# Moving the loads, casts and scores of an attention tail within a one-core kernel

## The chip, the core and the metric

The kernel runs on one core of a Trainium2 chip. The metric is device time in microseconds, the median of several runs. The core has five engines with a queue of their own each: TensorE (PE, with its weight loads as PEld), VectorE (DVE), ScalarE (ACT), GpSimd (POOL) and SyncE (SP). SyncE computes nothing here: it issues nearly all the DMAs, one after the other. Engines meet only by semaphores, so an instruction that waits holds up everything behind it on its engine.

## The reference

For 8 batches of 576 positions with 8 heads of 64 columns, the kernel computes sliding window attention and then a two-layer network with a residual:

```python
rel = pos[:, None] - pos[None, :]
mask = (rel >= 0) & (rel < 64)
scores = np.where(mask, q @ k.T / 8, -1e9)          # per batch and head
x = softmax(scores) @ v                              # (8, 576, 512) over all heads
xn = (x - mean(x)) / sqrt(var(x) + 1e-6) * g_ln
out = x + relu(xn @ w_ch1) @ w_ch2                   # 512 -> 2048 -> 512
```

## The kernel before

**Groups.** Rows go through the network in nine groups of 512. Groups 0 to 7 are the first 512 positions of batches 0 to 7. Group 8 (`NGRP - 1`) holds what is left, the last 64 positions of each batch. These are handled in four *tails* of two batches each; tail i belongs to batches 2i and 2i+1 and gives block i of group 8.

**A period.** The loop over `g` emits the network of group g (`mlp_units`) and, between its units, the attention of group g+1 and the loads and casts of group g+2. A unit is a piece of TensorE work: for g = 2 to 6 units 0 to 15 are layer 1 (one 128-row slice of the hidden layer each, `l1`, L498 and L502), units 16 to 29 are layer 2 as seven products of a Strassen scheme in two halves each (`stage`, in the order 4, 1, 2, 6, 5, 7, 3; L572). `at(i, f, ...)` puts a call behind unit i; calls behind the same unit run in the order in which `at` was called, and `at(40, ...)` means behind the last unit. So the order on every engine's queue is the order of these calls, written out by hand. No scheduler changes it.

**Attention of a block.** `load_qk` loads, `cast_qk` casts to 16 bits on GpSimd (or `cast_act` on ScalarE), `t_main` transposes (q of later batches by a DMA transpose from SyncE, L275, k on TensorE, L286), `s_pe` computes scores (L345), `s_exp` exponentiates (L355), `s_mask` multiplies by the mask on VectorE (L365), `b_pe` multiplies with v (L392), `b_rows` divides, writes the rows `xn` (L412, L416) and takes their statistics (L422, L425), `z_step` normalizes on GpSimd (L444 to L450), and `zt_step` transposes z into zT by a DMA transpose from SyncE (L470). `after_mask` (L358) is a one-element copy on GpSimd that reads a masked tile, so that GpSimd's later work waits for that mask product.

**A tail.** `load_tail` loads q (L107), k and v (L110); `cast_tail` casts q and k (L117, L118), `cast_tail_v` v (L124); `t_tail` transposes both by DMA (L302, L303). Scores and values run through the same `s_pe`, `s_exp`, `s_mask`, `b_pe` with group number 8.

**Around layer 2.** `s_sums` (L546) makes the Strassen sums sS of hidden rows on VectorE, in pieces of chunks. `post` (L585) and `post_both` (L581) add a product's bank into `xn`. Product 6 continues in the bank of product 1, so it waits for `post("A", 0, 0)`. `store` (L533) writes two blocks of `xn` behind product 7 and two behind product 3, the last two units. `xn` has four buffers of two blocks, so the first rows of group g+1 go where group g-1 was, and wait for its stores.

**Where the change lies.** In periods g = 3 to 6. In the kernel before, tail g-2 is loaded in period g (q and k behind unit 17, v at the end), q and k are cast behind unit 24, transposed by DMA at the end, and scored in period g+1 behind unit 13 (in g = 6 behind unit 9).

Of the kernel before, what the change touches and what calls it, by code (L numbers as in the profile page):

```python
# [18 lines left out]
def kernel(  # L19
# [15 lines left out]
    NGRP = B + 1  # L35
# [927 lines left out]
    for g in range(NGRP):  # L963
# [4 lines left out]
        units, s_sums = begun.get(g) or mlp_units(g, (8, 16, 16)[g] if g < 3 else 0, g == 0, g > 0)  # L968
        slots = [[] for _ in range(len(units) + 1)]

        def at(i, f, *a):
            slots[min(i, len(slots) - 1)].append((f, a))

        def first_scores(b, i):
            at(i, s_pe, b, 0)
            at(i, s_pe, b, 1, False, "xps")
            at(i, s_exp, b, 0, 0, 1)
            at(i + 1, s_exp, b, 1, 0, 1)
            at(i + 1, s_mask, b, 0)
            at(i + 2, s_mask, b, 1)  # L980
# [50 lines left out]
        if g == 1:  # L1031
# [38 lines left out]
            for j in range(4):  # L1070
                i = (13, 16, 22, 22)[j]
# [5 lines left out]
                i = (13, 17, 25, 27)[j]  # L1077
# [26 lines left out]
        if g == 2:  # L1104
            at(0, load_qk, 4, 1)
            at(0, s_exp, 3, 1, 1)
            at(1, z_act, 2, 3)
            at(1, s_mask, 3, 1)
            at(2, b_pe, 3, 0)
            at(2, s_pe, 3, 2)  # L1110
            at(2, s_pe, 3, 3, False, "t")
            at(5, zt_step, 2, 3, "act")
            for i, x in zip((2, 3, 4, 6), ((3, 0), (3, 1), (2, 0), (2, 1))):
                at(i, s_exp, 3, *x)
            at(3, load_v, 4, 0, 4)
            at(4, s_mask, 3, 3)
            at(4, b_rows, 3, 0)
            at(4, z_step, 3, 0)
            at(7, s_mask, 3, 2)
            at(7, alloc_qkT, 4)  # L1120
            at(7, after_mask, 3, 2)
            at(7, cast_qk, 4, 0)
            at(7, cast_qk, 4, 1)
            for j in range(1, 4):
                at(9, b_pe, 3, j, ("xps", "t", "sc")[j - 1])
                at((9, 10, 11)[j - 1], b_rows, 3, j)
                at((9, 10, 11)[j - 1], z_step, 3, j)
            for j, i in enumerate((8, 14, 24, 25)):
                at(i, zt_step, 3, j)
        elif g > 1 and b < B:  # L1130
            r, i = NGRP - 1, g - 3
            x, y = (b, 3), (r, i)
            at(2, b_pe, b, 0)
            at(2, b_rows, b, 0)
            at(2, z_step, b, 0)
            at(2, s_pe, b, 2)
            at(2, s_exp, b, 2, 0, 1)
            at(3, s_mask, b, 2)
            at(2, s_pe, *x, False, "t")
            at(4, s_exp, *x, 0)  # L1140
            at(5, s_exp, *x, 1)
            at(5, s_mask, *x)
            at(7, b_pe, b, 1)
            at(7, b_pe, *x, "t")
            if g == 6:
                at(9, s_mm, *y)
            at(7, b_rows, b, 1)
            at(7, z_step, b, 1)
            if g == 6:
                at(10, s_mask, *y)  # L1150
            at(8, b_rows, *x)
            at(9, z_step, *x)
            at(13, b_pe, b, 2)
            if g == 6:
                at(13, b_pe, *y, "sc")
            else:
                at(13, s_pe, *y)
                at(15, s_exp, *y, 0, 1)
                at(20, s_mask, *y)
            if g + 2 < B:  # L1160
                at(5, alloc_qkT, g + 2)
                at(5, after_mask, *x)
                at(5, cast_qk, g + 2, 0)
                at(5, cast_qk, g + 2, 1, (0,))
                at(15, cast_act, g + 2, 1, 1)
            for j, w in ((13, (b, 2)), (19, y)) if g == 6 else ((17, (b, 2)),):
                at(j, b_rows, *w)
                at(j, z_step, *w)
            at(2, zt_step, b, 0)
            at(14, zt_step, b, 1)  # L1170
            if g == 6:
                at(25, zt_step, r, i)
            at(16, zt_step, b, 3)
            at(18 if g == 6 else 17, zt_step, b, 2)
        n = g + 2
        if g > 1 and n < B:
            if g > 2:
                at(3, load_v, n, 2, 4)
            at(17, alloc_v, n)
            at(17, cast_v, n, 0, 2)  # L1180
            at(17, cast_v, n, 2, 4)
            if g == 2:
                at(26, part_vB, n, 0, 4)
            else:
                at(17, alloc_vB, n)
                for i, f, c in ((18, vB_cur, 0), (18, vB_prev, 0), (19, vB_cur, 1), (19, vB_prev, 1),
                                (24, vB_cur, 2), (24, vB_prev, 2), (24, vB_cur, 3)):
                    at(i, f, n, c, 0)
            for i, (x, half) in zip((13, 18, 13, 22) if g == 2 else (13, 17, 13, 23),
                                    ((0, 0), (1, 0), (0, 1), (1, 1))):  # L1190
                at(i, t_main, n, x, half, 0)
            if g > 2:
                at(23, b_pe, NGRP - 1, g - 3, "sc")
                at(23, b_rows, NGRP - 1, g - 3)
                at(23, z_step, NGRP - 1, g - 3)
            first_scores(n, 27)
            if n + 1 < B:
                for f, a in ((t_tail, (g - 2,)), (load_qk, (n + 1, 0)))[::1 if g == 2 else -1]:
                    at(40, f, *a)
                at(40, load_qk, n + 1, 1)  # L1200
                at(40, load_v, n + 1, 0, 2)
            else:
                at(40, t_tail, g - 2)
            if g > 2:
                at(40, zt_step, NGRP - 1, g - 3)
        if g == 2:
            for c, i in ((0, 13), (4, 16)):
                at(i, s_sums, c, c + 4, 1, 2)
# [1 line left out]
        if 2 < g < NGRP - 2:  # L1210
            for i in range(1, 5):
                at(7 + i, s_sums, 0, 4, i)
                at((13, 13, 18, 19)[i - 1], s_sums, 4, 6, i)
                at((15, 15, 20, 22)[i - 1], s_sums, 6, 8, i)
        if 2 <= g < 6:
            i = g - 2
            for n, part in enumerate("qkv"):
                at(15 if i == 0 else 40 if n == 2 else 17, load_tail, i, part)
            at(24, cast_tail, i)
        if 3 <= g < 7:  # L1220
            at(6 if g == 6 else 16, cast_tail_v, g - 3)
        if g == 5:
# [6 lines left out]
        if g in (6, 7):  # L1229
            i = 25 if g == 6 else 24  # L1230
# [40 lines left out]
```

## Time and profile before

| | us |
|---|---|
| median of three runs | 302.19 |
| the runs | 302.36, 302.19, 300.04 |
| the profiled execution, its own time | 299.51 |
| its span, first to last instruction | 297.8 |
| TensorE busy within the span | 289.3 |
| VectorE busy | 226.7 |
| ScalarE busy | 167.5 |
| GpSimd busy | 166.4 |

The profile is of one execution of the program. "Busy" is the time in which an engine ran at least one instruction, and lines are those of the kernel printed above. `out<-in` names what an instruction writes and reads. In brackets behind a row stand the idle time of the engine just before it and what ended it. For a DMA, the row on SPq is the issue; the landing comes later.

### The profile page before, as it was taken

The numbers are of one execution on the slowest core, as the hardware profiler recorded it, in microseconds if no ns is written. First come the engines' busy times: TensorE is split into PE (matmuls) and PEld (weight loads), VectorE is DVE, ScalarE is ACT, GpSimd is POOL, SyncE is SP. The second block draws the span as 40 slices with busy tenths as digits, with TensorE's granted clock in tenths as the row PEclk, the third lists the DMA queues.
The fourth block names the chain that finished last, engine by engine and source line by source line (L and its number), as shares of the span: only waits on it lengthen the run. The fifth ranks groups of instructions, "written<-read, shape, count | busy, mean of one in ns | idle before, by whom it ended". The sixth has DMA issues, their size and how long they took to land.

```text
span 297.8 us, 7948 instructions
## 1 busy us (share of the span) xinstructions
PE 289.3 (97%) x3207; PEld 210.7 (71%) x3207; DVE 226.7 (76%) x435; ACT 167.5 (56%) x284; POOL 166.4 (56%) x243
## 2 busy tenths in 40 slices
PE   8989999999999999999999999999979999999994
PEld 3558545898888888457854786468634888888883
DVE  2782378799994894498867785779869988988983
ACT  2667667677449625768577757776666117305500
POOL 4688866763850886257746883677456643104300
PEclk9999999999999999999999999999999999999999
DMA  8999999969979999899699999999693222003013
GB/s 189 258 382 341 384 293 285 258 207 299 195 165 274 254 156 216 226 307 170 135 273 272 186 141 279 271 200 189 132 226 69 53 77 84 4 0 144 0 37 106
DMA packets 116519, 57.63 MB, mean 194 GB/s; under 512 B 86273, under 2 KB 107841, under 8 KB 116482
## 3 DMA queue, kind: packets, MB, share of 16 engines
q1 hardware_dynamic: 116112, 56.79, 81.1%
q8 instruction: 25, 0.41, 0.6%
q10 hardware_dynamic: 370, 0.33, 0.3%
q14 instruction: 12, 0.10, 0.1%
HBM read 38.80 MB, written 9.44 MB: 162 GB/s over the span
## 4 chain that ended last, share of the span: by engine, by line
PE 91%; DVE 4%; DMA 1%; ACT 1%; issue 1%; SPq 0%; DVEq 0%
PE hps L498 19%; PE pA L572 14%; PE hph L641 12%; PE pC L572 10%; PE pB L572 9%; PE lA L697 5%; PE xps L392 4%; PE ch L658 4%; PE sc L345 3%; PE tp L286 3%; PE lC L697 2%; PE warm L887 2%; DMA out_dram<-xn 1%; PE ch L510 1%; PE lB L697 1%; PE ztp L474 1%
## 5 line engine op out<-in xcount | busy, mean ns | idle before, releaser
L498 PE MATMUL hps<-zT,w1g 128*128 128x512 f16 x288 | 66.2, 379 | 0.0
L502 ACT ACTIVATE hrT<-hps 128x512 f16<-128x512 f32 x72 | 43.2, 600 | 27.3 <-PE hps L498 22.5
L572 PEld LDWEIGHTS <-sS 128*128 128x128 f16 x512 | 49.1, 98 | 6.5 <-issue 0.5
L498 PEld LDWEIGHTS <-w1g 128*128 128x128 f16 x288 | 27.0, 98 | 30.7 <-issue 1.7
L355 ACT ACTIVATE pt<-sc 128x512 f16<-128x512 f32 x72 | 39.5, 601 | 15.2 <-PE sc L345 14.7
L572 PEld LDWEIGHTS <-hrT 128*128 128x128 f16 x384 | 36.7, 98 | 6.8 <-ACT hrT L502 0.8
L641 PE MATMUL hph<-zT,w1g 128*128 128x256 f16 x320 | 37.9, 273 | 0.0
L161 POOL CAST qk<-qk 128x1024 f16<-128x1024 f32 x26 | 28.0, 1091 | 13.7 <-PE sc L345 5.9
L365 DVE TENSOR_TENSOR pt<-pt,mask 128x1024 f16<-128x1024 f16 x32 | 24.6, 777 | 12.7 <-ACT pt L355 12.7
L641 PEld LDWEIGHTS <-w1g 128*128 128x128 f16 x320 | 30.5, 98 | 4.5 <-ACT w1g L238 0.2
L572 PE MATMUL pC<-w2s,sS 128*128 128x256 f16 x256 | 31.5, 273 | 0.0
L572 PE MATMUL pA<-wT,sS 128*128 128x256 f16 x256 | 30.9, 273 | 0.3 <-DVE xn L585 0.3
L444 POOL TENSOR_SCALAR rsz<-mvg 128x1 f32<-128x1 f32 x32 | 11.0, 342 | 36.1 <-DVE mvg L425 26.3
L646 ACT ACTIVATE hrT<-hph 128x512 f16<-128x512 f32 x40 | 24.1, 606 | 10.9 <-PE hph L641 10.6
L416 DVE TENSOR_TENSOR xn<-xps,rcp 128x256 f32<-128x256 f32 (+1 forms) x50 | 25.7, 538 | 4.7 <-DMA out_dram<-xn 4.1
L714 POOL TENSOR_SCALAR hrT<-hrT 128x512 f16<-128x512 f16 x8 | 12.0, 1503 | 28.5 <-DVE hrT L712 28.5
L546 DVE TENSOR_TENSOR sS<-hrT 128x1024 f16<-128x1024 f16 (+2 forms) x39 | 24.9, 639 | 3.2 <-ACT hrT L502 3.1
L267 ACT COPY qkT<-tp 128x1024 f16<-128x1024 f16 (+1 forms) x18 | 17.4, 965 | 16.0 <-PE tp L286 13.7
L422 DVE BATCH_NORM_STATS2 stats<-xn 128x6 f32<-128x512 f32 x36 | 25.0, 694 | 1.2
L445 POOL TENSOR_TENSOR rsz<-rsz,mhalf 128x1 f32<-128x1 f32 x32 | 21.0, 657 | 2.7
L450 POOL TENSOR_SCALAR z<-xn,rsz 128x512 f16<-128x512 f32 x24 | 20.6, 860 | 2.6 <-DMA zT<-z 0.2
L189 POOL CAST vA<-v 128x1024 f16<-128x1024 f32 (+1 forms) x18 | 17.3, 978 | 5.5 <-DMA v<-in_v_dram 5.4
(115 smaller groups left out, 486.9 us busy)
## 6 DMA issues: line engine op xcount, KB each, us to landing
qk<-in_q_dram SPq DMA_DIRECT2D x16, 512.0 KB, 6.0
qk<-in_k_dram SPq DMA_DIRECT2D x16, 512.0 KB, 6.3
out_dram<-xn SPq DMA_DIRECT2D x32, 256.0 KB, 4.1
v<-in_v_dram SPq DMA_DIRECT2D x28, 256.0 KB, 7.1
w2s<-in_moe_w_ch_dram SPq DMA_DIRECT2D x9, 512.0 KB, 8.4
w1s<-in_moe_w_ch_dram SPq DMA_DIRECT2D x4, 512.0 KB, 7.2
tk<-in_k_dram SPq DMA_DIRECT2D x8, 256.0 KB, 4.3
tv<-in_v_dram SPq DMA_DIRECT2D x8, 256.0 KB, 4.8
```

The costliest lines, as they stand in the source:

```text
L161: nc.gpsimd.tensor_copy(out=dst[:, :].rearrange("p (a j) e d -> p a e j d", j=j), in_=t[:, :].rearrange("p (a e j d) -> p a e j d", e=2, j ...
L355: nc.scalar.activation(out=o, in_=i, func=AF.Exp, bias=0.0, scale=scale)
L365: nc.vector.tensor_tensor(out=ptv, in0=ptv, in1=mb, op=ALU.mult)
L416: nc.vector.tensor_tensor(out=xn[:, n * i:n * i + n], in0=xps[:, :, 0:D], in1=rcp_b, op=ALU.mult)
L422: nc.vector.bn_stats(out=stats, in_=xv)
L498: nc.tensor.matmul(out=hps, lhsT=w1g[:, kc, 128 * hc:128 * (hc + 1)], rhs=zT[g][:, kc, :], start=(kc == 0), stop=(kc == NKC - 1),)
L502: nc.scalar.activation(out=hrT[:, hc, :], in_=hps, func=AF.Relu, bias=0.0, scale=1.0)
L546: nc.vector.tensor_tensor(out=o, in0=x, in1=y, op=op)
L572: nc.tensor.matmul(out=o, lhsT=a[:, c, 128 * p:128 * p + 128], rhs=wv[:, c, :], start=(first and (p == 0 or split_c) and c == 0), stop=(c ...
L641: nc.tensor.matmul(out=hps[:, e], lhsT=w1g[:, kc, 128 * hc:128 * (hc + 1)], rhs=zT[g][:, kc, 256 * half:256 * half + 256], start=(kc == 0) ...
L646: nc.scalar.activation(out=hrT[:, 2 * i:2 * i + 2, 256 * half:256 * half + 256], in_=hps, func=AF.Relu, bias=0.0, scale=1.0)
L697: nc.tensor.matmul(out=o[:, r, :], lhsT=a[:, kc, 2 * d + r, :], rhs=b[:, kc, :], start=(n in (1, 2, 5) and r == 0 and kc == 0), stop=(kc = ...
```

## The change

Tails 1 to 3 (tail 0 stays) are handled one step later. q and k of a tail are loaded behind the stores at the end of a period, ahead of the next q/k loads, and not ahead of the stores; at the end of g = 5 v as well. Their cast and transpose move to the next period behind unit 2, after z of block 0. The zT transpose of the tail block before goes there too. The load of the next v (first half) and of the tail's v move from the end of a period to behind unit 2 of the next. A tail's scores come behind unit 17 in place of 13, ahead of the k transposes (in g = 6 behind 13 in place of 9, with its value product behind 18). A cast of q (second half) on GpSimd goes from unit 5 to 11. One piece of the sum sS number 3 goes from unit 18 to 19, so it stands behind the add of product 1.

```diff
         elif g > 1 and b < B:
             r, i = NGRP - 1, g - 3
             x, y = (b, 3), (r, i)
+            if g > 3:
+                at(2, zt_step, r, i - 1)
             at(2, b_pe, b, 0)
             at(2, b_rows, b, 0)
             at(2, z_step, b, 0)
+            if g > 3:
+                at(2, cast_tail, i)
+                at(2, t_tail, i)
+                if g < 6:
+                    at(2, load_v, g + 2, 0, 2)
+                    at(2, load_tail, i, "v")
...
-            if g == 6:
-                at(9, s_mm, *y)
...
-            if g == 6:
-                at(10, s_mask, *y)
...
+            i_s = 13 if g == 6 else 17
+            at(i_s, s_pe, *y)
+            at(i_s + 2 if g == 6 else i_s, s_exp, *y, 0, 1)
             if g == 6:
-                at(13, b_pe, *y, "sc")
+                at(15, s_mask, *y)
+                at(18, b_pe, *y, "sc")
             else:
-                at(13, s_pe, *y)
-                at(15, s_exp, *y, 0, 1)
                 at(20, s_mask, *y)
...
-                at(5, cast_qk, g + 2, 1, (0,))
+                at(11, cast_qk, g + 2, 1, (0,))
...
             if n + 1 < B:
-                for f, a in ((t_tail, (g - 2,)), (load_qk, (n + 1, 0)))[::1 if g == 2 else -1]:
-                    at(40, f, *a)
+                if g == 2:
+                    at(40, t_tail, 0)
+                else:
+                    at(40, load_tail, g - 2, "q")
+                    at(40, load_tail, g - 2, "k")
+                at(40, load_qk, n + 1, 0)
                 at(40, load_qk, n + 1, 1)
-                at(40, load_v, n + 1, 0, 2)
+                if g == 2:
+                    at(40, load_v, n + 1, 0, 2)
             else:
-                at(40, t_tail, g - 2)
-            if g > 2:
-                at(40, zt_step, NGRP - 1, g - 3)
+                for part in "qkv":
+                    at(40, load_tail, g - 2, part)
...
-                at((13, 13, 18, 19)[i - 1], s_sums, 4, 6, i)
+                at((13, 13, 19, 19)[i - 1], s_sums, 4, 6, i)
...
         if 2 <= g < 6:
             i = g - 2
-            for n, part in enumerate("qkv"):
-                at(15 if i == 0 else 40 if n == 2 else 17, load_tail, i, part)
-            at(24, cast_tail, i)
+            if i == 0:
+                for part in "qkv":
+                    at(15, load_tail, i, part)
+                at(24, cast_tail, i)
```

## The prediction

> **What bounds the kernel now.** I read the page's busy shares first, then busy time by stretches, then TensorE's waits, then the timeline around each wait. A group is a "period" of some 31 us: 16 units of layer 1, then 14 units of layer 2. g=4 runs from 149.8, g=5 from 180.8, g=6 from 212.3.
>
> ```profile
> PE 289.3 (97%) x3207; PEld 210.7 (71%) x3207; DVE 226.7 (76%) x435; ACT 167.5 (56%) x284; POOL 166.4 (56%) x243
> ...
> 149.99:180.96 30.97, 30.97 (x354) 20.59 (x352) 23.12 (x48) 21.73 (x38) 19.79 (x29) 1.00 1.10 215
> 180.96:212.26 31.30, 30.96 (x352) 20.51 (x351) 25.24 (x50) 21.55 (x38) 21.40 (x30) 1.00 1.10 218
> 212.26:243.00 30.74, 28.97 (x301) 18.64 (x299) 25.72 (x53) 12.89 (x24) 16.14 (x24) 1.00 0.52 114
> 243.00:268.00 25.00, 24.96 (x227) 21.85 (x225) 22.06 (x40) 9.24 (x17) 6.05 (x4) 1.00 0.12 43
> ```
>
> ```profile
> PE xps L392 <- DVE pt L365: 1.8, 1, 1.8
> PE pA L572 <- DVE xn L585: 0.3, 1, 0.3
> ```
>
> The columns of the stretches are length, then busy time of PE, PEld, DVE, ACT and POOL, then clock, DMA share and GB/s. TensorE sets the time, at a granted clock of 1.00. Period g=4 has no idle TensorE time at all. Period g=5 is 0.34 us short (31.30 against 30.96 busy), g=6 1.77 us short, and after 243 there is 0.04 us in 25. Matmuls are not removed by this change, so what it can gain in the periods it touches ends at 0.34 + 1.77 = 2.1 us. That is under 1% of the time. About 1% is also what a measurement of this kernel can tell from no change, since the three runs shown lie 2.3 us apart.
>
> **The large wait, 1.77 us in g=6.**
>
> ```profile
> 210.50 1.22 DVE L581 TENSOR_TENSOR xn<-pA,xn 128x1024 f32<-128x1024 f32 x1
> 211.63 1.25 SPq L110 DMA_DIRECT2D tk<-in_k_dram  x2
> 212.98 2.75 SPq L533 DMA_DIRECT2D out_dram<-xn  x4
> 215.47 0.21 DVE L412 RECIPROCAL rcp<-xps 128x8 f32<-128x8 f32 x1 [0.58 <-PE xps L392]
> 218.06 0.69 DVE L416 TENSOR_TENSOR xn<-xps,rcp 128x512 f32<-128x512 f32 x1 [2.39 <-DMA out_dram<-xn]
> 219.31 0.62 ACT L355 ACTIVATE pt<-sc 128x512 f16<-128x512 f32 x1
> 221.93 0.68 DVE L365 TENSOR_TENSOR pt<-pt,mask 128x1024 f16<-128x1024 f16 x1
> 222.67 0.22 PE L392 MATMUL xps<-vB,pt 128*64 128x65 f16 x1 [1.77 <-DVE pt L365]
> ```
>
> Group 5's result is complete at 211.72 (210.50 + 1.22). SyncE is then still issuing tail loads and gives the first store at 212.98. VectorE's multiply for the next group needs the stored buffer, and waits 2.39 us for that landing. Everything behind it on VectorE is late, the last mask product ends at 222.61, and TensorE waits for that one.
>
> After the change the stores come first: 212.98 - 211.72 = 1.26 us earlier. They also no longer queue behind four fresh loads. I take 2.4 us off the multiply (the whole wait; lower bound 1.26). The mask product would then end near 222.61 - 2.4 = 220.2, if its exponent allows. That exponent ends at 219.93 (219.31 + 0.62), so the product ends at 220.6 at the earliest. TensorE wants it at 222.67 - 1.77 = 220.9. So 1.77 us goes with a margin of 0.3 us; at the lower bound 1.26 us goes. Next late would be that exponent.
>
> **The small wait, 0.34 us in g=5.**
>
> ```profile
> 170.91 0.39 DVE L546 TENSOR_TENSOR sS<-hrT 128x512 f16<-128x512 f16 x1
> ...
> 201.69 1.04 POOL L124 CAST vt<-tv 128x1024 f16<-128x1024 f32 x1 [1.41 <-DMA tv<-in_v_dram]
> ...
> 201.88 1.13 DVE L546 TENSOR_TENSOR sS<-hrT 128x512 f16<-128x512 f16 x1
> 202.93 0.68 DVE L585 TENSOR_TENSOR xn<-pA,xn 128x512 f32<-128x512 f32 x1
> ...
> 203.66 1.91 PE L572 MATMUL pA<-wT,sS 128*128 128x256 f16 x16 [0.34 <-DVE xn L585]
> ```
>
> The half sum took 0.39 us in g=4 and 1.13 us in g=5, where GpSimd's cast of the tail's v ran at the same time. The add behind it came late and TensorE waited. With the half sum behind the add, the add starts 1.05 us earlier (202.93 - 201.88). The 0.34 us goes, and nothing waits for that half sum until product 7, four units on. I count -0.34.
>
> **What is moved on TensorE: dearer by 0.1 us a period.** The tail's 16 score matmuls leave a place between layer-1 matmuls and come between layer-2 products and transposes.
>
> ```profile
> 133.37 0.41 PE L345 MATMUL sc<-tqT,tkT 64*128 64x64 f16 x16
> 133.71 1.90 PE L498 MATMUL hps<-zT,w1g 128*128 128x512 f16 x8
> ...
> 143.90 1.92 PE L572 MATMUL pC<-w2s,sS 128*128 128x256 f16 x16
> 145.66 1.91 PE L572 MATMUL pA<-wT,sS 128*128 128x256 f16 x16
> 147.50 0.64 PE L345 MATMUL sc<-qkT,qkT 64*128 64x64 f16 x32
> ```
>
> From start to start the scores cost 0.34 us where they stand (133.71 - 133.37). At the new place the step from 128x256 products into scores is dearer: a product ahead of scores holds 1.84 us (147.50 - 145.66), one ahead of a product 1.76. That is 0.08 a period, in g=3, 4 and 5. In g=6 the tail's 16 value matmuls also lose their neighbours of the same form, of the same order. Sum +0.3; bounds 0 and 0.7 (the scores' 0.34 twice).
>
> **What is moved on GpSimd: the tail casts get between z and the mask product.** Before, the one-element copy that waits for the last mask product stands between z of block 0 and the next casts. Now two tail casts stand ahead of that copy.
>
> ```profile
> 156.64 0.76 POOL L450 TENSOR_SCALAR z<-xn,rsz 128x512 f16<-128x512 f32 x1
> 157.53 0.69 DVE L365 TENSOR_TENSOR pt<-pt,mask 128x1024 f16<-128x1024 f16 x1 [2.04 <-ACT pt L355]
> 158.27 0.20 PE L392 MATMUL xps<-vB,pt 128*64 128x65 f16 x1
> ...
> 148.78 0.61 POOL L117 CAST tq<-tq 128x512 f16<-128x512 f32 x1 [0.85 <-DMA tq<-in_q_dram]
> ...
> 183.75 1.04 POOL L118 CAST tk<-tk 128x1024 f16<-128x1024 f32 x1 [0.99 <-DMA tk<-in_k_dram]
> ```
>
> GpSimd is free at 157.40, the mask product starts at 157.53, ends at 158.22, and TensorE uses its result at 158.27: a margin of 0.05 us. The g=5 half sum showed what a GpSimd cast does to such a VectorE operation: it holds it until the cast is over. If the q cast of 0.61 us gets in first, the product ends about 0.5 us late and TensorE waits as long; if the product gets in first, nothing is lost. The two starts lie 0.1 us apart, so I count half of three periods, 3 x 0.5 / 2 = about +0.7 us; bounds 0 and 3 x (0.61 + 1.04) = 5.0, when both casts get ahead.
>
> [...]
>
> **What is moved on SyncE and the DMA queue: the transposes get tighter.**
>
> ```profile
> 150.00:175.00 25.00, 25.00 (x274) 15.48 (x273) 18.83 (x41) 17.22 (x31) 17.04 (x25) 1.00 1.23 238
> 175.00:180.00 5.00, 5.00 (x73) 4.31 (x72) 3.60 (x8) 3.55 (x7) 2.75 (x6) 1.00 0.48 101
> ...
> 177.18 1.29 SPq L107 DMA_DIRECT2D tq<-in_q_dram  x2
> ...
> tq<-in_q_dram SPq DMA_DIRECT2D x8, 128.0 KB, 3.1
> ...
> L303 SPq DMA_TRANSPOSE tkT<-tk x1: 2713/2713/2713, 154.3 to 154.3; - x1
> DMA to landing us min/median/max: 5.7/5.7/5.7
> ...
> L470 SPq DMA_TRANSPOSE zT<-z x1: 1216/1216/1216, 175.9 to 175.9; - x1
> DMA to landing us min/median/max: 2.3/2.3/2.3
> ...
> 168.25 0.61 PE L286 MATMUL tp<-ident,qk 128*128 128x128 f16 x8
> ```
>
> Before, the four tail loads ran in the quiet end of a period (share 0.48). Now they stand at the head of the busy 25 us (1.23). Issued from 177.18, the last one let GpSimd's cast start at 183.75; taking off the 3.1 us that a single q load takes to land, they hold the queue some 3.5 us. The tail's k transpose landed at 160.0 (154.3 + 5.7). In front of it now come these 3.5 us and two more q/k loads, 1.05 MB at 238 GB/s, 4.4 us at most. It lands at 168 or earlier; TensorE scores the tail at 168.25 - 0.34 = 167.9. So it is close: I take 0 for the likeliest, since the stores ahead land sooner than before; bounds 0 and 1 us in each of g=4 and g=5. Queued behind it on SyncE are the v loads, the group's q transposes and its zT. Before, the last zT of g=4 landed at 178.2 (175.9 + 2.3), 2.6 us ahead of the next period's first product at 180.8; later loads eat into that as well. On ScalarE a cast of k now waits for the same transpose; it stands after layer 1's last evacuation, so only the q/k copies are behind it.
>
> The remaining edits cost nothing that I can find. The second q cast goes from unit 5 to unit 11 of GpSimd's queue, and its transpose is used behind unit 27; the tail's v load moves within the queue; tail 0 is loaded as before.
>
> **Sum** against the profiled execution (299.51 us, span 297.8): -1.77 - 0.34 + 0.3 + 0.7 + 0 = -1.1, so 298.4. The median of the runs shown, 302.19, lies 2.7 above that execution. I carry the same -1.1 to it: 301.1.
>
> **Rivals.**
> - *Nothing collides* (the mask product gets the port first each time): -2.1 + 0.3 = -1.8, 300.4. For it speaks that the cast also needs its q landed and the two starts lie 0.1 us apart; against it the 0.05 us margin.
> - *Both casts ahead of the mask product, the slower side.* Place: around 8 us into g=4, 5 and 6. Price 1.65 us each, 5.0 in all, minus 1.8: +3.2, 305.4. It decides from 0.6 us a period on. For it: GpSimd's second cast follows its first at once if k has landed. Against: a waiting VectorE operation should get its turn between two casts.
> - *The tail transposes come late* (1 us in g=4 and g=5 each): -1.8 + 0.7 + 2 = +0.9, 303.1. Decided by a landing past 167.9.
> - *The change doesn't do what it says:* the store wait goes, but mask or exponent stays as late, so only 0.3 of the 2.1 goes and the 1.0 of costs stays: 302.9.
>
> **Chances.** Forecast (-0.5 to -1.7) 0.45, nothing collides 0.2, late transposes 0.15, both casts ahead 0.1, no gain 0.1. Over 1% faster needs 3 us, more than all idle time there is; only spread of the runs gives it: 0.05. Over 1% slower: the port rival and a part of the late transposes, 0.12. Within 1%: 0.83. The range reaches from the full gain with runs like the lowest (300.04 - 1.8 = 298.2) up to between the late transposes and the port rival, 304.0.
>
> **What would show it.** TensorE's wait for the mask product at the start of g=6 gone or under 0.5 us; no VectorE wait for a store in xn<-xps; the half sum behind the add and no wait of pA. A wait of TensorE for the mask product some 8 us into g=4 and g=5, with a long mask product beside the tq cast, shows the port. A wait at the tail's scores for the transposes, or at a period's first layer-1 matmul for zT, shows the DMA queue. The forecast is wrong if either is over 0.7 us a period.

## The result, and the profile after

In the first comparison the changed kernel took 299.24 us (median of 15 executions, 298.63 to 300.96), the kernel before 301.86 (15 executions, 300.04 to 303.62). The ratio is 0.9923, 95% interval 0.9901 to 0.9945, so it is 0.8% or some 2.3 us faster (2.6 us by the medians). Ratios here leave out executions over 1.5% above the fastest of the same kernel; of the kernel before that takes out 23 of 112 in the groups below, all at a mean granted clock of 0.994 or less. The forecast was 301.1, range 298.2 to 304.0.

The two profiled executions compare the wrong way round: that of the changed kernel was the slowest of its 15 (300.96), that of the kernel before (299.51) was faster than any of its 15. So the profile after shows where time goes, not how much goes in a typical execution. Busy time by periods in the changed kernel, from each period's first layer-1 matmul to the next (columns as in the prediction):

```profile
149.68:183.65 33.97, 31.73 (x355) 20.63 (x353) 24.56 (x50) 22.03 (x38) 19.12 (x30) 1.00 1.09 209
183.65:215.48 31.83, 31.46 (x353) 20.64 (x353) 24.82 (x49) 21.69 (x37) 20.36 (x30) 1.00 1.08 224
215.48:243.35 27.87, 27.75 (x291) 17.64 (x290) 25.64 (x53) 12.54 (x23) 15.53 (x25) 1.00 0.64 128
```

The waits have changed places. Before, g=4 had no idle TensorE time and g=6 had 1.77 us; now g=4 has 2.24 us (33.97 - 31.73), g=5 0.37, g=6 0.12. TensorE's waits say for what:

```profile
PE sc L345 <- DMA qkT<-qk: 1.3, 2, 0.8
...
PE hps L498 <- issue: 0.6, 1, 0.6
...
PE sc L345 <- DMA tkT<-tk: 0.3, 1, 0.3
```

The first and the third are DMA transposes. The second is a period's first layer-1 matmul, which needs zT: the profile names no releaser, but the last zT transpose of g=4 is issued at 181.2 and these take 2.3 to 2.5 us to land, and the matmul starts at 183.65. The waits for the mask product at the start of g=6 and for the add of pA are gone. The timeline there shows the store as the prediction had it:

```profile
214.42 1.21 DVE L581 TENSOR_TENSOR xn<-pA,xn 128x1024 f32<-128x1024 f32 x1
...
215.66 2.03 SPq L533 DMA_DIRECT2D out_dram<-xn  x4
...
218.69 0.21 DVE L412 RECIPROCAL rcp<-xps 128x8 f32<-128x8 f32 x1
218.93 0.69 DVE L416 TENSOR_TENSOR xn<-xps,rcp 128x512 f32<-128x512 f32 x1
...
223.18 0.69 DVE L365 TENSOR_TENSOR pt<-pt,mask 128x1024 f16<-128x1024 f16 x1 [0.30 <-ACT pt L355]
```

The result is complete at 215.63 and the store goes out at 215.66, no longer 1.26 us later. The multiply follows its reciprocal without a wait (2.39 us before). The last mask product now waits for its exponent, which the prediction named as next late.

### The profile page after: what moved, and what is told of

It reads as the page before. It is cut to its first block, busy times and chain, and to the rows that moved or that the text cites. A ratio compares the mean times of both kernels' runs of the same rounds, so it can differ in the third digit from the quotient of the medians.

```text
span 299.2 us, 7940 instructions
## 1 busy us (share of the span) xinstructions
PE 289.2 (97%) x3207; PEld 210.0 (70%) x3207; DVE 227.8 (76%) x435; ACT 168.2 (56%) x284; POOL 164.1 (55%) x243
## 4 chain that ended last, share of the span: by engine, by line
PE 75%; DMA 10%; DVE 4%; SPq 3%; ACT 2%; POOL 2%; issue 2%; POOLq 0%
PE hps L498 14%; PE hph L641 12%; PE pA L572 11%; PE pC L572 8%; PE pB L572 7%; PE lA L697 5%; PE ch L658 4%; DMA tkT<-tk 3%; PE sc L345 3%; PE xps L392 3%; PE tp L286 3%; PE lC L697 2%; DMA qk<-in_k_dram 2%; DMA tk<-in_k_dram 2%; DMA tv<-in_v_dram 2%
## 5 line engine op out<-in xcount | busy, mean ns | idle before, releaser
L365 DVE TENSOR_TENSOR pt<-pt,mask 128x1024 f16<-128x1024 f16 x32 | 25.2, 795 | 15.8 <-ACT pt L355 15.8
L161 POOL CAST qk<-qk 128x1024 f16<-128x1024 f32 x26 | 28.9, 1120 | 11.9 <-DMA qk<-in_q_dram 7.9
L450 POOL TENSOR_SCALAR z<-xn,rsz 128x512 f16<-128x512 f32 x24 | 21.2, 882 | 2.6 <-DMA zT<-z 0.2
```

Of the source, the lines that this page charges most:

```text
L161: nc.gpsimd.tensor_copy(out=dst[:, :].rearrange("p (a j) e d -> p a e j d", j=j), in_=t[:, :].rearrange("p (a e j d) -> p a e j d", e=2, j ...
L365: nc.vector.tensor_tensor(out=ptv, in0=ptv, in1=mb, op=ALU.mult)
```

## The experiments

All ratios are against the kernel before, run on the same chip in the same group. In the four groups it took 301.70, 301.34, 301.35 and 301.39 us.

**Both kernels once more.**

> The kernel before once more, unchanged. Its profiled execution so far (299.51 us) was 2.35 us faster than its median (301.86). If that spread comes from the DMA queue (landings of transposes that now and then come late), a second profiled execution near 301 to 302 us shows more waits of TensorE for qkT, tkT or zT than the first one, which had none in the periods g=4 to g=6, and the same 0.3 us wait of pA and 1.8 us wait for the mask product. If the spread sits elsewhere (start, end, clock), the periods g=4 to g=6 last 30.97, 31.30 and 30.74 us again.

Measured: 302.58 us (298.68 to 304.98), ratio 1.0012 (0.9966 to 1.0058). The unexpected thing is the clock that each execution lists. Of the 89 executions of the kernel before that the ratios keep, 49 have a mean granted clock of 0.997 or more and a median of 300.1 us; 40 have 0.994 or less and a median of 302.1. The profiled execution took 303.62 us at a clock of 0.988. It has no wait of TensorE for qkT, tkT or zT, and one of 3.4 us for the mask product in g=6, so in this execution it isn't the late transposes, which the expectation named first, that cost the time. No price below is taken from it.

> The changed kernel once more, unchanged. Its profiled execution so far (300.96 us) was its slowest of 15, with waits of TensorE for the tail's k transpose (0.3 us), the group's q transposes (1.34 us) and zT (0.65 us) in g=4. DMA theory: these waits are chance, so an execution near the median of 299.24 us has at most 0.5 us of them in all, and the ratio to the kernel before is 0.990 to 0.995. Rival, that the waits belong to the change: they come back at the same place with the same 2 to 3 us in g=4, whatever the time.

Measured: 299.43 us (298.30 to 301.21), ratio 0.9936 (0.9906 to 0.9966). All 27 executions of the changed kernel so far have a clock of 0.997 or more. The profiled one is again the slowest of its run (301.21); its waits:

```profile
PE sc L345 <- DMA tkT<-tk: 1.2, 2, 0.7
...
PE sc L345 <- DMA qkT<-qk: 0.3, 1, 0.3
```

The same kinds of waits come in other places and sizes: for tkT 0.7 us in g=5 and 0.5 in g=6, and under 0.1 us of waiting in g=4. So the rival falls. The first expectation holds for the ratio; its 0.5 us for an execution near the median isn't tested by one that is so far above it.

**The store order.** The q and k loads go back behind unit 17:

```diff
-                    at(40, load_tail, g - 2, "q")
-                    at(40, load_tail, g - 2, "k")
+        if 3 <= g < 6:
+            at(17, load_tail, g - 2, "q")
+            at(17, load_tail, g - 2, "k")
```

> The changed kernel with the q and k loads of tails 1 to 3 back behind unit 17, ahead of the stores; all else stays as changed. Store theory: the wait of VectorE's multiply for the store comes back at the start of g=6 and with it 1.3 to 1.8 us of TensorE's wait for the mask product; the four loads also no longer stand in front of the transposes, so tkT and qkT land some 3 us earlier and no wait for them is seen. Sum about 299.2 + 1.5 = 300.7 us, ratio to before 0.994 to 0.999. Rival, that the place of the loads in the queue does not matter to the store wait (that it was the half sum or the tail's v load): no wait over 0.5 us at the start of g=6, and a time at or under that of the changed kernel.

Measured: 300.32 us (298.38 to 303.05), ratio 0.9984 (0.9947 to 1.0021). The wait is back. Timeline and stretches of this run:

```profile
211.30 1.25 SPq L110 DMA_DIRECT2D tk<-in_k_dram  x2
...
212.64 2.79 SPq L533 DMA_DIRECT2D out_dram<-xn  x4
...
217.69 0.69 DVE L416 TENSOR_TENSOR xn<-xps,rcp 128x512 f32<-128x512 f32 x1 [2.55 <-DMA out_dram<-xn]
...
222.30 0.22 PE L392 MATMUL xps<-vB,pt 128*64 128x65 f16 x1 [1.93 <-DVE pt L365]
```

```profile
222.30:226.30 4.00, 4.00 (x25) 1.66 (x26) 3.83 (x11) 0.72 (x2) 3.81 (x7) 0.57 0.16 33
223.00:226.00 3.00, 3.00 (x9) 1.08 (x8) 2.86 (x10) 0.60 (x1) 2.91 (x6) 0.50 0.22 44
```

The last column but two is the clock. Behind the wait of 1.93 us TensorE runs at half clock for 4.00 x 0.43 / 0.5 = 3.4 us, which costs 1.7 us on top of the wait. Six of the twelve executions have a clock of 0.993 or less and a median of 301.9; the other six have 299.1. So the store order is the cause of the wait, and in this run the wait cost its length of 1.93 us or, with the half clock behind it, almost twice that (1.93 + 1.7 us). What it is worth in time is known less well: the run is 0.9 us above the changed kernel of the same group by the medians and 1.4 by the ratios, whose intervals overlap.

**The price of the loads.** Both kernels without the q and k loads of tails 1 to 3:

```diff
+        if i > 0 and part != "v":
+            ...
+            tail32[i].append(keep[part])
+            return
```

> The changed kernel without the q and k loads of tails 1 to 3 (768 KB for each tail left out; tail 0's rows are used in their place, so the rows of group 8 are not those of the reference). DMA theory: what the changed kernel loses in its typical run is the queue in front of tkT, qkT and zT; without these loads their waits vanish and the time falls by 0.5 to 1.5 us below the changed kernel, to about 298.2 us, with a smaller spread of the runs. Rival, that these transposes are in time in a typical run and the loss is elsewhere (port, scores, start): the time stays within 0.4 us of the changed kernel.

> The kernel before without the q and k loads of tails 1 to 3 (768 KB for each left out, tail 0's rows used in their place, so the rows of group 8 are not those of the reference). These are the loads that stand ahead of the stores. Store theory: without them the stores start 1.26 us earlier and land sooner, VectorE's waits for a store in g=5 and g=6 shrink to under 0.5 us, TensorE's wait for the mask product goes, and with it every stretch at half clock: all executions at a mean clock of 0.997 or more, median 298.2 to 299, ratio 0.988 to 0.993, with a spread under 1.5 us. Rival, that the late store and the low clock have another cause (the v loads, the transposes): the wait of 1 to 2 us stays and the median is above 300.

Measured: the changed kernel without them 298.21 us (298.06 to 299.38), ratio 0.9927 (0.9897 to 0.9957), 1.2 us below the changed kernel in the same group. The kernel before without them 297.25 us (297.08 to 297.90), ratio 0.9891 (0.9841 to 0.9942), 4.1 us below and under the 298.2 to 299 expected, all six executions at a clock of 0.999 or more. In neither profile does TensorE wait over 0.1 us for a mask product, tkT, qkT or zT. So these loads cost 1.2 us where they stand now, and 4.1 us by the medians where they stood (3.3 by the ratio, whose interval is 1.7 to 4.8): about twice the 1.77 us wait of the one profiled execution.

Without the loads the order is the other way round: the changed one is slower by 0.96 us. That is what the rest of the change costs, with some doubt: the two runs are of different chips, on which the kernel before differs by 0.35 us the same way, and between the two profiled executions it is 0.55 us from g=3 on. Periods g=4 and g=5, first of the kernel before without the loads, then of the changed one:

```profile
149.77:181.07 31.30, 31.12 (x355) 20.63 (x353) 23.95 (x49) 21.73 (x38) 19.43 (x30) 1.00 1.02 202
181.07:212.03 30.96, 30.96 (x355) 20.63 (x353) 24.40 (x51) 21.73 (x38) 20.33 (x30) 1.00 0.99 204
```

```profile
149.75:181.09 31.34, 31.25 (x354) 20.63 (x352) 24.19 (x48) 21.83 (x38) 20.07 (x30) 1.00 1.05 202
181.09:212.43 31.34, 31.25 (x354) 20.62 (x352) 25.52 (x50) 21.83 (x38) 21.41 (x30) 1.00 1.01 202
```

In g=5 the difference is 31.34 - 30.96 = 0.38 us. In g=4 it is only 0.04; a wait of 0.18 us for the add in the kernel before explains about half of that. The difference in g=5 has two parts. One is what the recorded texts call the port: a cast on GpSimd and VectorE's mask product at the same time, where one of the two takes longer. These are the mask product and the value products behind it, from the start of the first to the next layer-1 matmul, in g=4 of the changed kernel, and then of the kernel before:

```profile
157.21 0.61 POOL L117 CAST tq<-tq 128x512 f16<-128x512 f32 x1
157.38 0.98 DVE L365 TENSOR_TENSOR pt<-pt,mask 128x1024 f16<-128x1024 f16 x1 [2.04 <-ACT pt L355]
...
157.86 0.22 PE L392 MATMUL xps<-vB,pt 128*64 128x65 f16 x1
...
158.80 0.39 PE L498 MATMUL hps<-zT,w1g 128*128 128x512 f16 x1
```

```profile
158.02 0.22 PE L392 MATMUL xps<-vB,pt 128*64 128x65 f16 x1
...
158.66 1.25 PE L498 MATMUL hps<-zT,w1g 128*128 128x512 f16 x5
```

The q cast starts 0.17 us ahead, the mask product takes 0.98 us in place of 0.69, and TensorE passes the value products in 0.94 us in place of 0.64. It is 0.27 to 0.30 us in each of g=4 and g=5; in g=6 the cast comes after the mask product and costs nothing. In the changed kernel without the loads the k cast follows the q cast at once, and it is the k cast that is held, 1.50 us in place of 1.04, while the mask product takes no longer than with the q cast alone (0.97 us):

```profile
157.82 1.50 POOL L126 CAST tk<-tk 128x1024 f16<-128x1024 f32 x1
```

So in this run the waiting VectorE operation got its turn between the two casts, as the prediction argued against its rival "both casts ahead". The gap that the trace marks is only 0.1 us, since the rest hides in the modelled ends of the matmuls: the step from start to start tells more than the wait. The other part is the scores' new place. The product ahead of them, in the kernel before and in the changed one without the loads:

```profile
166.41 2.01 PE L572 MATMUL pB<-wT,hrT 128*128 128x256 f16 x16
168.25 0.61 PE L286 MATMUL tp<-ident,qk 128*128 128x128 f16 x8
```

```profile
166.26 2.01 PE L580 MATMUL pB<-wT,hrT 128*128 128x256 f16 x16
168.20 0.41 PE L353 MATMUL sc<-tqT,tkT 64*128 64x64 f16 x16
```

1.94 against 1.84 us: 0.1 us a period.

**The clock alone.** In the kernel before, matmuls of zeros fill the wait:

```diff
-            at(7, b_pe, *x, "t")
+            at(7, b_pe, *x, "t", 7 if g == 6 else 0)
```

> The kernel before, with seven matmuls of zeros (128x512, some 0.22 us each, 1.5 us in all) put ahead of the value product of g=6 for which TensorE waits 1.77 us or more; they write the bank that this product then overwrites. Nothing else is moved, so the store comes as late as before. [...] Rival, that the slow executions of the kernel before come from a later store alone: clock or not, the median stays within 0.5 us of the kernel before, or rises.

Measured: 301.28 us (300.20 to 302.46), ratio 1.0023 (0.9992 to 1.0055). Eleven of twelve executions have a clock of 0.997 or more, so with the fill the clock stays up; the median didn't fall, so the time didn't follow. The profiled execution (300.83) has its loss one period earlier:

```profile
187.77 0.69 DVE L420 TENSOR_TENSOR xn<-xps,rcp 128x512 f32<-128x512 f32 x1 [3.14 <-DMA out_dram<-xn]
```

The same store wait, 0.95 us in the first profile of the kernel before, is 3.14 us here in g=5, and TensorE waits 0.8 us for that mask product and 0.4 for the add of pA. The fill also takes its 1.5 us where the wait would have been shorter; how often that is wasn't measured. So this run does not show what the clock is worth, and the rival isn't excluded by it.

**The scores back behind unit 13,** all else as changed, gives TensorE a long wait in another place:

```diff
-            i_s = 13 if g == 6 else 17
+            i_s = 13
```

> The changed kernel with the tail's scores back behind unit 13, all else as changed. DMA theory: the tail's k transpose lands at about 168, the scores would start at about 164.5, so TensorE waits some 3 us in each of g=4 and g=5 (6 us in all). [...] Rival, that the low clock behind the mask product's wait was something else: the clock stays at 0.997 or more and the time rises by 6 us, to 305.

Measured: 309.32 us (307.95 to 311.06), ratio 1.0296 (1.0241 to 1.0351), all six executions at a clock of 0.989 or less, so the rival with its 305 us at 0.997 or more falls. Waits and stretches:

```profile
PE sc L345 <- DMA tkT<-tk: 7.1, 3, 4.1
```

```profile
165.50:168.14 2.64, 0.01 (x3) 0.01 (x2) 1.50 (x4) 0.27 (x1) 2.27 (x5) 0.86 0.91 194
168.14:175.00 6.86, 6.86 (x43) 3.89 (x44) 1.57 (x2) 3.19 (x6) 3.66 (x6) 0.56 1.35 227
175.00:181.00 6.00, 6.00 (x65) 5.45 (x62) 5.72 (x13) 3.49 (x5) 3.00 (x5) 1.00 0.68 141
```

A wait of 2.6 us in g=4, and half clock for (2.64 x 0.14 + 6.86 x 0.44) / 0.5 = 6.8 us (the clock is 0.50 all the way from 169 to 174); the first 0.7 us of it lie in the wait itself. The same again in g=5: 6.8 us, with 4.1 us of wait. That is twice the 3.4 us behind the wait of 1.93 us in the run with the loads first. So in these runs the low clock comes with a wait of TensorE, for the mask product in one and for tkT in the other. It doesn't come with each: behind the wait of 1.77 us, in the first profile of the kernel before, the clock was 1.00. What decides it isn't shown.

**The half sum back in front of the add.**

```diff
-                at((13, 13, 19, 19)[i - 1], s_sums, 4, 6, i)
+                at((13, 13, 18, 19)[i - 1], s_sums, 4, 6, i)
```

> The changed kernel with the half sum back in front of the add (behind unit 18), all else as changed. As predicted, TensorE waits 0.3 us for the add in g=5, where GpSimd's cast of the tail's v runs beside the half sum: 0.3 us above the changed kernel. Rival, that the tail's v now lands at another time and its cast no longer meets the half sum: no wait of the product's bank and no difference that can be measured.

Measured: 299.27 us (298.25 to 299.82), ratio 0.9923 (0.9892 to 0.9955), beside 0.9936 and 0.9923 with the edit. No wait of pA. Its g=5:

```profile
203.01 0.39 DVE L546 TENSOR_TENSOR sS<-hrT 128x512 f16<-128x512 f16 x1
203.32 0.68 DVE L585 TENSOR_TENSOR xn<-pA,xn 128x512 f32<-128x512 f32 x1
204.50 1.34 POOL L124 CAST vt<-tv 128x1024 f16<-128x1024 f32 x1 [2.25 <-DMA tv<-in_v_dram]
```

The cast of the tail's v now starts 1.1 us after the half sum has ended. In the changed kernel its load stands further back in SyncE's order, and that alone parts the two. The rival held.

**The loads between the two pairs of stores** (behind unit 27 in place of 40).

> The changed kernel with the tail's q and k loads behind unit 27, between the two pairs of stores, in place of behind the last store. DMA theory: these loads then start some 1.2 us earlier in each period, the tail's k transpose and what is queued behind it land as much earlier, and the executions lose some 0.3 to 0.8 us less than the changed kernel (299.4 in these runs), about 298.8; the store for which the next rows wait is of the pair behind the loads or ahead of it: if behind, a wait of TensorE for the mask product in g=6 of 0.5 to 1 us comes back. Rival, that the loads only swap places with the stores in the same queue: within 0.3 us of the changed kernel.

Measured: 300.76 us (298.73 to 301.72), ratio 0.9978 (0.9947 to 1.0008). Slower than the changed kernel (299.27 us for the run just above, on the same chip), so the earlier start of the loads gains nothing. In g=5 the tail's v too now stands ahead of the second pair of stores, and VectorE waits 2.55 us for a store ahead of the rows of block 3 in g=6 (first fence). TensorE's wait in g=6 is another, 1.3 us for tkT (second); it also waits 0.5 us for qkT and 0.6 at a layer-1 matmul. That the late store brings these about isn't shown.

```profile
227.57 0.76 DVE L416 TENSOR_TENSOR xn<-xps,rcp 128x256 f32<-128x256 f32 x2 [2.55 <-DMA out_dram<-xn]
```

```profile
PE sc L345 <- DMA tkT<-tk: 1.3, 1, 1.3
```

**The tail's casts behind the mask product.**

```diff
-                at(2, cast_tail, i)
-                at(2, t_tail, i)
+                at(5, after_mask, *x)
+                at(5, cast_tail, i)
+                at(5, t_tail, i)
```

> The changed kernel with the casts and transposes of tails 1 to 3, and the loads of v that follow them on SyncE, behind the copy that waits for the mask product, so that no cast can get in front of it. Port theory as predicted: 0.5 us in half of three periods comes back, 0.7 us in all, 298.7. As the two traces of the changed kernel have it (0.1 us in each of g=4 and g=5): 0.2 to 0.3 us, less what the transposes lose by starting some 1 us later; within 0.4 us of the changed kernel, on either side. DMA theory: the later transposes make the waits for tkT and qkT longer and the time rises by 0.3 to 1 us.

Measured: 301.51 us (300.37 to 303.08), ratio 1.0013 (0.9984 to 1.0042). The value products are at 0.65 us again in g=4 and g=5, but the time is 2.2 us above the run with the half sum back, on the same chip, more than the 0.3 to 1 us that the DMA theory gave. In the profiled execution the transposes of g=4 are issued 1.2 to 2.7 us later than in the changed kernel's two, and TensorE waits for tkT in each of g=4 to g=6:

```profile
PE sc L345 <- DMA tkT<-tk: 2.4, 3, 1.4
```

**Half of the group's loads behind the tail's transposes,** alone and with the casts behind the mask product:

```diff
                 at(2, t_tail, i)
                 if g < 6:
+                    at(2, load_qk, g + 2, 1, (1, 0))
```

> The changed kernel with the second half of the next q and k loads (the last two of the four that stand ahead of the tail's transposes, 1 MB) moved behind the tail's transposes, k first. DMA theory: the transposes no longer wait for these two loads, the tail's k transpose lands 2 to 4 us earlier, its waits in g=4 to g=6 go, SyncE comes free earlier for zT and the q transposes, and the time falls by 0.5 to 1 us, to about 298.6. Rival: the two loads now land after ScalarE's cast of k asks for them (167.7 in g=4), ScalarE waits, TensorE with it, and the time rises by 1 us or more.

> The changed kernel with the second half of the next q and k loads behind the tail's transposes, and in g=4 and g=5 also the tail's casts, transposes and those loads behind the copy that waits for the mask product (g=6 as changed). Port theory: in the traces of the changed kernel the mask product takes 0.98 us beside the q cast in place of 0.69, and the value products behind it 0.92 us from start to start in place of 0.65; with the cast behind it both are 0.69 and 0.65 again, 0.27 us in each of two periods. DMA theory: the transposes now have 2 to 3 us to spare, so a start some 0.8 us later costs nothing. Sum 299.4 - 0.5, about 298.9, ratio 0.989 to 0.994. Rival: the later casts push GpSimd's z, and the waits for tkT, zT or the q transposes come back as in the run with the casts behind the mask product (0.4 to 1.5 us a period): 300 or more.

Measured: 299.58 us (298.73 to 300.20), ratio 0.9954 (0.9924 to 0.9984), the changed kernel's time again; and 301.11 us (299.84 to 302.56), ratio 1.0012 (0.9983 to 1.0040). In SyncE's rows the k transpose of g=4 is issued earlier and faster, at 159.81 in 1.64 us (first fence), than in the changed kernel (second):

```profile
159.81 1.64 SPq L304 DMA_TRANSPOSE tkT<-tk  x1
```

```profile
162.15 3.72 SPq L303 DMA_TRANSPOSE tkT<-tk  x1
```

The wait for tkT goes, but what is queued behind gains little: against the run with the half sum back, v is issued 2 us earlier, the tail's v then takes 4.0 us to issue in place of 2.0, and the q transposes and the last zT are 0.5 and 0.2 us earlier. A 0.34 us wait at the layer-1 matmul that needs zT stays, and neither the gain nor the loss expected came. With the casts moved too, the time is over the rival's 300, and the tail's v is the longest wait:

```profile
PE xps L393 <- POOL vt L125: 0.7, 1, 0.7
```

That is 0.7 us, and 0.5 us at the first layer-1 matmul of g=5; the rest of the 1.5 us between the two runs, which are of different chips, isn't found. No complete version tried beats the changed kernel.

## Why the prediction was right, and where it was not

The direction, the range and "within 1%" held. The predicted gain of 1.1 us was half of the measured one, which lies outside the -0.5 to -1.7 that the chances gave the forecast. The terms behind it were off in both directions, so that the total came as near as it did is partly luck. The prices are those of the runs above, from different groups and chips, so the sum is rough.

| term | predicted | measured |
|---|---|---|
| store wait | -1.77 | -3.3 to -4.1, of the loads ahead of the stores in the kernel before, wait and clock together |
| half sum | -0.34 | 0 |
| scores' new place | +0.3 | +0.1 a period, three periods |
| port | +0.7 | +0.27 to 0.30 in each of two periods, about +0.56 |
| DMA queue | 0 | +1.2 |
| sum | -1.1 | -1.2 to -2.0 (ratio of the kernels: -1.9 and -2.3) |

That this sum meets the measured gain is no proof of its terms. From the kernel before, through the two runs without the loads, to the changed kernel is a chain, and its steps by the medians (-4.1, +0.96 and +1.2) must add up to the gain. What is checked independently is the middle step: port and scores make 0.86 us in the traces, against 0.96. And put back in the changed kernel ahead of the stores, the same loads cost 2.1 us over the run without them (1.7 by the ratios), at the lower end of the 1.7 to 4.8 that they cost in the kernel before. So the split among the terms is open; that the late store and the low clock are gone isn't.

- **The store wait** was the right mechanism, mis-sized. The step that failed is "so 1.77 us goes": it took the wait from a fast execution as if it were typical, and took a wait to cost only its length. In three profiles with the loads ahead of the stores VectorE waits 0.95 to 3.14 us for a store in g=5 and 2.25 to 2.55 in g=6. And 40 of 89 executions had a low clock, with a median 2.0 us higher. The prediction read the clock of 1.00 and didn't ask what a longer wait would do to it. Most of the 4.1 us is there without the low clock: in that group the seven executions of the kernel before at 0.997 or more have a median of 299.98 us, 2.7 above the run without the loads. How the rest divides between longer waits and the clock stays open, since the fill didn't separate them.
- **The half sum** held its place in the profile but not its price. "I count -0.34" missed that another edit, the later load of v, already takes the cast away from it.
- **The port** came out near the sum, by another way. It isn't 0.5 us in half of three periods: in g=4 and g=5 of the changed kernel's two profiles the cast is first, by 0.17 to 0.19 us, and costs 0.3. In g=5 of the kernel before the mask product is first, by 0.03 us (181.60 against 181.63): it takes its 0.68 us, and the q cast 1.12 in place of 0.61. So in these cases the one that starts first keeps its time and the other takes longer. The prediction read from the half sum that the cast holds the VectorE operation until it is over, and the changed kernel's trace shows less: from the recorded end of the cast on, the mask product would have ended 1.13 us after its start (157.82 + 0.69 - 157.38), and it took 0.98.
- **The scores** cost what the step from product to scores gave, 0.1 against 0.08 us.
- **The DMA queue.** The estimate that tkT lands "at 168 or earlier" in g=4 was near: it landed at 168.3 (162.1 + 6.2) in the first profile of the changed kernel and at 168.2 in the second. The choice of 0 was wrong. The prediction worked out g=4 alone, but in g=5 TensorE waits 0.3 and 0.7 us for tkT in these profiles, and the q transposes and zT behind it are as tight: the largest wait is 1.3 us for qkT. A margin of nothing is a cost when landings vary from one execution to the next. The prediction's own sign of being wrong, over 0.7 us a period for tkT or zT, was just reached (0.72). Of the rivals, late transposes held as a cost of 1.2 us, within its bound of 2; it was outweighed by a store term larger than thought. "Nothing collides" is nearest in time (a gain of 1.8), but the q cast and the mask product did collide, in g=4 and g=5. "Both casts ahead" and "doesn't do what it says" didn't occur.

## What to carry to other kernels

Before pricing a wait from one profile, see where that execution stands among the others, and look at the clock that each of them lists: here a wait of 1.93 us on TensorE cost 1.7 us more in the stretch behind it. Loads that nobody needs soon belong behind a store that somebody waits for, but what queues behind them then pays (these loads cost 3.3 to 4.1 us ahead of the stores and 1.2 us behind them); taking the loads out of both kernels for a run gives a price for each place, though what a load costs may also depend on the other edits around it. When two edits cure the same collision, only one of them can be paid for it.

## What the runs showed of the hardware

- TensorE fell to half clock (0.50) for 3.4 us behind a wait of 1.93 us, and for 6.8 us with waits of 2.6 and 4.1 us, of which the first 0.7 and 1.4 us lay in the waits themselves. A wait of 1.77 us in another execution had a clock of 1.00 behind it.
- In one stretch the DMA engines were busy and moved almost nothing. In the changed kernel's profiled execution, with SyncE issuing the group's q transposes, the mean engine share is 1.70 and the rate 13 GB/s (the last two columns):

```profile
176.00:178.00 2.00, 2.00 (x21) 1.79 (x19) 1.84 (x4) 1.30 (x3) 1.70 (x2) 1.00 1.70 13
```

The stretch is just ahead of the landings for which TensorE then waited 1.3 us. It is one execution, and what brings it about wasn't tried.
- The issue of the k transpose of g=4 on SyncE took 1.64 us with two loads fewer ahead of it, and 3.29, 3.60 and 3.72 us with them in three executions. In these four executions the issue time of this transpose went with what was queued ahead of it, and the time saved on the transpose came back at the tail's v (4.0 us of issue in place of 2.0).
